# Values two units behind scores in the first chunk, and six decode and halving steps earlier, in a sparse attention and feed-forward kernel on one Trainium2 core

## The chip, the cores and the metric

The kernel runs on one core of a Trainium2 chip. TensorE (PE) does the matmuls, VectorE (DVE) and ScalarE (ACT) the elementwise work, GpSimd (POOL) copies, and SyncE (SP) issues almost all transfers. The metric is device time in microseconds (us), the median of the runs shown. Less is better.

## The reference

Attention over 4 batches, 8 heads, 768 positions and 64 numbers per head, with a mask by blocks of 32 positions, and a feed-forward layer behind it:

```python
scores = scale * np.matmul(q, k.transpose(0, 1, 3, 2))
mask = np.abs(blk_i - blk_j) <= 1
mask = mask | (blk_i == 0) | (blk_j == 0) | (blk_i == 23) | (blk_j == 23)
# and three sampled key blocks for each query block
scores = np.where(mask, scores, -1e9)
attn = softmax(scores)
x = (attn @ v).transpose(0, 2, 1, 3).reshape(3072, 512)
h = x @ w_in                       # 512 -> 2048
g = h * erf(softplus(h))
out = g @ w_out                    # 2048 -> 512
```

Everything is float32 outside. Inside, most matmuls take each factor as two float16 halves, a high one and a low one.

## The kernel before

**Units.** Each batch of attention is cut into 16 units. Units 0 to 9 of the first batch are the middle rows: unit n is row tile t = n // 2 (128 query positions) and quad n % 2 (four of the eight heads); in names of tiles, `pT_m_3_1` is tile 3, quad 1, so unit 7. Units 10, 11, 13, 14 (`f`) and 12, 15 (`e`) are the first and last blocks. For a unit, `scores` multiplies queries with gathered keys on PE into the one score bank `s`, `soft_max` takes maxima on DVE, `soft_exp` exponentiates on ACT (`pf`), `soft_low` makes the low halves on DVE (`p`), and `soft_turn` transposes the probabilities into `pT` by a DMA transpose that SP issues. `values` multiplies `pT` with gathered value blocks `vb` on PE into `po_bank`, and `norm` divides by the sum on DVE (`rinv`, `xf`). After a tile's second quad `turn` splits the rows (`x`) and has SP transpose them into `xT`.

**Groups.** The feed-forward layer runs in chunks of two tiles, each cut into 8 groups of two 128-wide slices of the hidden layer. The main loop runs over groups m; chunk 0 is m = 0 to 7 and chunk 1 m = 8 to 15. A group does `ff_first` (24 matmuls of `xT` with `w_in`, tile `h`), the logs and exponentials on ACT (`ff_logs`, `ff_exp`), a group later the gate on DVE (`ff_gate`, tile `g`), and two groups later `ff_second` (12 matmuls into `o` for each chunk). In its groups a chunk also starts units: `begun` counts them, from 4 at m = 0, one for each group of chunks 0 and 1. `scores` of unit `begun` and `values` of unit `begun - PV_LAG` (three) stand in the same group. So group m of chunk 0 scores unit 4 + m and takes the values of unit 1 + m, from unit 4 on. Units 0 to 3 are done in front of the loop.

**Gathers of values.** `vb` has 8 slots, four for a tile. When `values` of a tile's second quad is in the program, `gathers` issues the next tile's value blocks on SP: 14 transfers for a middle tile, 11 for the last blocks and two wholes.

**Weights.** They come as 64-bit words and are decoded in place: `D` (`decode_pair`, three DVE passes over two of the 16 pieces), `Q` (squares on ACT for the scale), `A` and `B` (sum over the squares, scale), `H` (`split_hi`, high halves on ACT) and `L` (`split_lo`, low halves on DVE). `i` is `w_in`, `o` is `w_out`, and the digit is the pair. The high halves of a pair are written over the pair before it, so `Hi3` needs `Li2`. `ff_first` of groups 0 and 1 needs pairs 0 and 1 of `w_in`, groups 2 and 3 need pairs 2 and 3, and so on. `Do2` and `Do3` also make POOL issue the loads of pairs 4 and 5 of `w_out`. The tables `EARLY`, `AMID` and `LATE` say which steps stand in which group, early (behind `scores`, the gate and `norm`, in front of `ff_second`), in the middle (behind `soft_exp`) and late (at the end).

**Order.** Every engine works through its instructions in the order of the program, which is written out by hand. SP's transfers each wait, in that order, for the transfer eight places earlier on the queue to have landed. In group 1, ACT's squares of the next batch's first value piece (`vj`, of tile `vraw`) stand in front of `soft_exp` of unit 5.

Of the kernel before, what the change touches and what calls it, by code (L numbers as in the profile page):

```python
# [24 lines left out]
H_CAP = 4.4  # L25


EARLY = ("", "", "Ao Bo Ho0 Lo0", "Hi5", "Hi6", "Hi7")
AMID = ("Do3 Qo1 Qo2", "Do5", "", "Li5 Lo2", "Li6 Lo3", "Li7 Lo4", "Lo5", "Lo6", "Lo7")
LATE = (  # L30
    "Qo3 Do4 Hi2 Li2 Qo4 Hi3 Li3",
    "Qo5 Do6 Qo6 Do7 Qo7",
    "Hi4 Ho1 Li4 Lo1 Ho2",
    "Ho3",
    "Ho4",
# [8 lines left out]
def sparse_attention_moe(ctx: ExitStack, tc: tile.TileContext, qT, kT, v, sampled, w_in, w_out, out):  # L44
# [38 lines left out]
    PV_LAG = 3  # L83
# [54 lines left out]
    def load_q(b, t):  # L138
        place, tag, bufs = (mo, "g", FF_LAG + 1) if b == 0 and t in (1, 2) else (ld, "qt", 2)
        qt = place.tile([P, HP, P], F32, tag=tag, name=f"qt_{b}_{t}", bufs=bufs)  # L140
        rows = qT[b].rearrange("(r t) d s -> (t d) r s", t=2)
        if t < MT:
            c = (1 + 4 * t) * BLOCK
            sp.dma_start(qt, rows[:, :, c : c + P])
        else:
            sp.dma_start(qt[:, :, : 3 * BLOCK], rows[:, :, S - 3 * BLOCK :])
            sp.dma_start(qt[:, :, 3 * BLOCK :], rows[:, :, :BLOCK])
        qts[b, t] = qt
# [114 lines left out]
    def write_values():  # L263
        for write in writes:
            sp.dma_start(*write)
        writes.clear()
# [272 lines left out]
    def work(steps):  # L539

        for step in steps.split():
            kind, key, k = step[0], step[1], step[2:]
            steps_of[kind](key, *([int(k)] if k else []))
# [274 lines left out]
    def write_results():  # L818
        for result in results:
            sp.dma_start(*result)  # L820
        results.clear()
# [21 lines left out]
    def gathers(m):  # L843

        nonlocal vfree
        gather_keys()
        room = 4 if begun > 0 else VGS
        while vjobs and vjobs[0][0] in have_v:
            b, i = vjobs[0]
            n = 2 if i > 0 else 1  # L850
            fresh = b > 0 and 0 < i < VGS
            if vfree < n or room < n * (1 + fresh):
                break
            vfree -= n
            room -= n * (1 + fresh)
            vjobs.pop(0)
            gather_v(b, i) if i > 0 else whole_v(b, -1 - i)
# [9 lines left out]
    def behind(m):  # L867

        b, n = divmod(m, per)
        if b + 1 < B:  # L870
            c = b + 1
            if n == 10:
                load_q(c, 0)
            k = n - 4 if b else 2 * (n - 10) if n > 9 else -1
            if k in ((1, 3, 5, 7) if b else (2, 4, 6, 8)):
                order_k(c, (k - 1) // 2)
            if k in (0, 2, 4, 6):
                load_k(c, k // 2)
            if k == 8:
                have_k.add(c)  # L880
            pr, k = divmod(n - 3, 3)
            if pr in range(HP):
                if k == 0:
                    load_v(c, pr)
                if k == 1:
                    prepare(square_v, None, (c, pr))
                if k == 2:
                    prepare(scale_v, None, (c, pr))
                    prepare(high_v, low_v, (c, pr))
                    if pr == HP - 1:  # L890
                        prepare(None, join_scales, (c,))
            if pr == HP and k == 0:
                have_v.add(c)
# [7 lines left out]
    def seen(unit):  # L901

        if unit[0] == "m":
            return unit[1:]
        if unit[0] == "e":
            return unit[1], MT, unit[2]
        return None

    def used_keys(unit):
        nonlocal kfree  # L910
        if unit[0] == "m" and unit[3] == 1:
            kfree += 4
        elif unit[0] == "e" and unit[2] == 1:
            kfree += 4

    FIRST = 4
    begun = 0

    def unit_of(n):
        return units[n] if 0 <= n < len(units) else None

    def values_of(place, *halves):
        nonlocal vfree
        values(*place, *halves)
        if place[2] == 1 and halves != ((0,),):
            vfree += 4 if place[1] < MT else 5
# [92 lines left out]
    work("Do2")  # L1021
    gathers(0)
    load_q(0, 3)
    begun = FIRST
    behind(begun - 1)

# [5 lines left out]
    for m in range(len(groups) + FF_LAG):  # L1032
        ch, i = divmod(m, NGR)
        steps = 0
        if ch < len(until):
            first = until[ch - 1] if ch else FIRST
            steps = first + -(-(until[ch] - first) * (i + 1) // NGR) - begun
        elif begun < len(units) + PV_LAG:
            steps = 1
        assert steps in (0, 1)  # L1040
        group = groups[m] if m < len(groups) else None
        last = groups[m - 1] if 0 < m <= len(groups) else None
        unit = unit_of(begun) if steps else None
        old = unit_of(begun - PV_LAG) if steps else None
        place = seen(old) if old and begun - PV_LAG >= FIRST else None
        begun += steps
        write_values()
        write_results()
        if group:
            ff_first(*group)  # L1050
            ff_logs(*group)
        ready, prepared[:] = prepared[:], []
        twice = bool(place) and place[1] == MT and m >= FF_LAG
        if place:
            values_of(place, *[(0,)] * twice)
        for high, _ in ready:
            if high:
                high()
        if twice:
            ff_second(*groups[m - FF_LAG], 0)  # L1060
            values_of(place, (1,))
        if steps:
            gathers(begun)
        if unit:
            scores(unit)
            used_keys(unit)
            gather_keys()
        if last:
            ff_gate(*last)
        if place:  # L1070
            norm(*place)
        if m < len(EARLY):
            work(EARLY[m])
        if m >= FF_LAG:
            for u in range(int(twice), CT):
                ff_second(*groups[m - FF_LAG], u)
        if unit:
            soft_max(unit)
            next_queries(begun - 1)
        if group:  # L1080
            ff_power(*group)
        for _, low in ready:
            if low:
                low()
        if unit:
            soft_exp(unit)
        if group:
            ff_exp(*group)
        if m < len(AMID):
            work(AMID[m])  # L1090
        if m >= FF_LAG:
            for u in range(CT):
                ff_store(*groups[m - FF_LAG], u)
        if unit:
            soft_low(unit)
            soft_turn(unit)
        if place:
            turn(*place)
        if m < len(LATE):
            work(LATE[m])  # L1100
        if unit:
            behind(begun - 1)
# [37 lines left out]
```

## Time and profile before

| | us |
|---|---|
| median of 3 runs | 808.74 (808.31 to 812.43) |
| the profiled execution | 805.82 |
| its span | 804.1 |

| engine | busy in the span, us | share |
|---|---|---|
| PE, matmuls | 698.1 | 87% |
| DVE | 571.2 | 71% |
| ACT | 550.8 | 69% |
| POOL | 120.8 | 15% |

The profiled execution is 2.92 us shorter than the median of the runs. Busy shares are averages over stages that differ: in front of the main loop, and in its first groups, PE waits for weights and transfers; later it hardly waits. So stages have to be read apart. Times in the rows are us from the span's start; a value in brackets is the idle time of that engine just before, and what ended it.

### The profile page before, as it was taken

To read this page: it belongs to the slowest core of one execution; us is meant where nothing else is said; L and a number is where in the kernel's file an instruction comes from. 1 tells how busy PE (TensorE), PEld (TensorE's weight loads), DVE (VectorE), ACT (ScalarE), POOL (GpSimd) and SP (SyncE) were. 2 spreads that over 40 slices of the span, in tenths; PEclk is the share of its full clock that TensorE was granted. 3 is DMA by queue.
4 is the path that set the end of the run, shared out by engine and by line. 5 is a ranking of instruction groups with operands and counts; after the bars stand their busy time and mean duration, and the time that the engine had idled before them with its cause. 6 is when DMAs were issued, how large, how long until landed. Compare 5 with 4: busy or idle time off the path is not lost.

```text
span 804.1 us, 26682 instructions
## 1 busy us (share of the span) xinstructions
PE 698.1 (87%) x10868; PEld 462.2 (57%) x10868; DVE 571.2 (71%) x1025; ACT 550.8 (69%) x943; POOL 120.8 (15%) x340
## 2 busy tenths in 40 slices
PE   2345646887998799999999999999999999999996
PEld 1234423544665566665666766666666666666663
DVE  3896687884877586886777848977768777654543
ACT  4654657984665577776767858876677776667674
POOL 4711211101311210210111111011111110000000
PEclk9999757998999899999999999999999999999999
DMA  8998972586979878893567998955677897410000
GB/s 312 280 285 269 288 169 63 126 191 140 186 157 179 204 184 196 190 235 63 145 162 149 236 189 166 234 125 126 134 174 149 179 176 190 67 42 2 14 28 26
DMA packets 200779, 129.24 MB, mean 161 GB/s; under 512 B 144080, under 2 KB 167760, under 8 KB 200656
## 3 DMA queue, kind: packets, MB, share of 16 engines
q1 hardware_dynamic: 197808, 117.83, 62.9%
q0 software_dynamic: 2848, 9.71, 3.8%
q8 instruction: 85, 1.39, 0.7%
q14 instruction: 38, 0.31, 0.1%
HBM read 81.52 MB, written 12.95 MB: 117 GB/s over the span
## 4 chain that ended last, share of the span: by engine, by line
PE 69%; DVE 10%; DMA 9%; ACT 5%; issue 4%; SPq 3%; POOL 0%; POOLq 0%; ACTq 0%; DVEq 0%
PE o L60 27%; PE h L60 27%; PE po_bank L60 6%; PE s_m L60 5%; SPq L60 3%; DMA vb<-vtab 3%; DVE keys L60 3%; PE s_f L60 3%; DMA vraw<-in_v_dram 2%; ACT x L60 1%; DVE wi L60 1%; ACT pf_m L60 1%; DMA keys<-in_w_out_dram 1%; DVE p_m L60 1%; DMA kr<-in_kT_dram 1%
## 5 line engine op out<-in xcount | busy, mean ns | idle before, releaser
L60 PE MATMUL h<-xT,wi 128*128 128x256 f16 x2304 | 277.5, 278 | 19.6 <-ACT wi L60 7.9
L60 PE MATMUL o<-wo,g 128*128 128x512 f16 x1152 | 270.2, 383 | 5.9 <-ACT wo L60 3.6
L60 PEld LDWEIGHTS <-wi 128*128 128x128 f16 x2304 | 228.7, 100 | 72.5 <-ACT wi L60 9.4
L60 PEld LDWEIGHTS <-g 128*128 128x128 f16 x1152 | 108.1, 99 | 142.5 <-issue 26.9
L60 ACT ACTIVATE x<-x 128x512 f32<-128x512 f32 x288 | 181.5, 630 | 9.2
L60 POOL COPY keys<-keys 128x128 f32 x264 | 90.2, 392 | 358.1 <-PE s_m L60 311.5
L60 ACT ACTIVATE x<-h,isg 128x512 f32<-128x512 f32 x96 | 66.0, 687 | 89.1 <-PE h L60 87.8
L60 DVE SCALAR_TENSOR_TENSOR q<-x,q 128x512 f32<-128x512 f32 x96 | 68.1, 710 | 59.2 <-ACT x L60 59.2
L60 ACT ACTIVATE pf_m<-s_m,nb_m 128x256 f32<-128x256 f32 x160 | 62.6, 473 | 51.5 <-DVE nb_m L60 48.6
L60 DVE SCALAR_TENSOR_TENSOR q<-q,h 128x512 f32<-128x512 f32 x96 | 65.4, 681 | 27.5 <-ACT q L60 27.5
L60 PE MATMUL s_m<-keys,qt 64*32 64x192 f32 (+1 forms) x1600 | 70.1, 352 | 7.7 <-ACT pf_m L60 4.9
L60 ACT ACTIVATE q<-q 128x512 f32<-128x512 f32 x96 | 60.5, 631 | 21.9 <-DVE q L60 21.8
L60 DVE SCALAR_TENSOR_TENSOR g<-q,g 128x512 f16<-128x512 f32 x96 | 66.5, 692 | 3.3
L60 ACT ACTIVATE q<-x 128x512 f32<-128x512 f32 x96 | 60.5, 630 | 3.0
L60 DVE TENSOR_REDUCE mx_m<-s_m 128x4 f32<-128x1024 f32 x40 | 48.8, 1220 | 19.0 <-PE s_m L60 18.5
L60 PEld LDWEIGHTS s_m<-keys,qt 64*32 64x32 f32 (+1 forms) x1600 | 45.5, 133 | 19.7 <-ACT pf_m L60 6.0
L60 PE MATMUL po_bank<-vb,pT_m 128*32 128x65 f16 (+1 forms) x3840 | 44.8, 201 | 12.5 <-DMA vb<-vtab 8.7
L60 DVE TENSOR_TENSOR p_m<-pf_m,p_m 128x1024 f16<-128x1024 f32 x40 | 49.0, 1226 | 4.6 <-ACT p_m L60 3.5
L60 PEld LDWEIGHTS <-pT_m 128*32 128x32 f16 x3840 | 38.0, 97 | 23.4 <-issue 13.3
L60 DVE TENSOR_SCALAR g<-q 128x512 f16<-128x512 f32 x96 | 41.1, 428 | 3.3
L60 DVE CAST p_m<-pf_m 128x1024 f16<-128x1024 f32 x30 | 20.9, 697 | 25.3 <-ACT pf_m L60 25.3
L60 POOL COPY keys<-wi 128x768 f32<-128x768 f32 (+1 forms) x24 | 14.4, 627 | 121.7 <-DMA wi<-in_kT_dram 115.6
(111 smaller groups left out, 528.1 us busy)
## 6 DMA issues: line engine op xcount, KB each, us to landing
vb<-vtab SPq DMA_DIRECT2D x280, 65.0 KB, 3.1
vb<-vtab SPq DMA_DIRECT2D x32, 390.0 KB, 4.4
vtab<-vn SPq DMA_DIRECT2D x16, 390.0 KB, 5.1
vb<-vtab SPq DMA_DIRECT2D x12, 520.0 KB, 5.2
qt<-in_qT_dram SPq DMA_DIRECT2D x20, 256.0 KB, 3.3
out_dram<-wo SPq DMA_DIRECT2D x20, 256.0 KB, 2.6
vb<-vtab SPq DMA_DIRECT2D x36, 130.0 KB, 3.4
vraw<-in_v_dram SPq DMA_DIRECT2D x12, 384.0 KB, 4.4
```

Of the source, the lines that this page charges most:

```text
L60: done = call(*args, **kwargs)
```

## The change

Two things move; no instruction is added but the order.

1. `values` runs two units behind `scores` instead of three while `begun` is under 12, that is in chunk 0; at m = 8 (`begun` 12) no values run; from m = 9 on it is three again. So units 4 to 9 have their values, their `norm` and their `turn`, and the gathers that follow, one group earlier (m = 2 to 7 instead of 3 to 8).
2. `Do3`, `Hi2`, `Li2`, `Hi3` and `Li3` go from groups 0 and 1 to the place in front of group 0; `Do4` to `Do6` each move up by half a group or so; `Do7`, `Qo6` and `Qo7` go from the end of group 1 into group 2, in front of `Ao`.

```diff
-EARLY = ("", "", "Ao Bo Ho0 Lo0", "Hi5", "Hi6", "Hi7")
-AMID = ("Do3 Qo1 Qo2", "Do5", "", "Li5 Lo2", "Li6 Lo3", "Li7 Lo4", "Lo5", "Lo6", "Lo7")
+EARLY = ("", "", "Qo6 Do7 Qo7 Ao Bo Ho0 Lo0", "Hi5", "Hi6", "Hi7")
+AMID = ("Do4 Qo1 Qo2", "Do6", "", "Li5 Lo2", "Li6 Lo3", "Li7 Lo4", "Lo5", "Lo6", "Lo7")
 LATE = (
-    "Qo3 Do4 Hi2 Li2 Qo4 Hi3 Li3",
-    "Qo5 Do6 Qo6 Do7 Qo7",
+    "Qo3 Do5 Qo4",
+    "Qo5",
...
+    NEAR = 12
...
     load_q(0, 3)
+    work("Do3 Hi2 Li2 Hi3 Li3")
     begun = FIRST
...
-        old = unit_of(begun - PV_LAG) if steps else None
-        place = seen(old) if old and begun - PV_LAG >= FIRST else None
+        due = begun - (PV_LAG - 1 if begun < NEAR else PV_LAG)
+        old = unit_of(due) if steps and begun != NEAR else None
+        place = seen(old) if old and due >= FIRST else None
```

**DVE at the head of the main loop.** `keys` is the decode's scratch, `wo<-wo,keys` the last pass of a `Do`, `wi<-wi,s_wi` an `Li`, `mx` the maxima of unit 4. Before:

```order
L60 SCALAR_TENSOR_TENSOR wo<-wo,keys 128x1024
L60 TENSOR_REDUCE mx_m_2_0_1203<-s_m_2_0_1182 128x4
L60 TENSOR_SCALAR nb_m_2_0_1205<-mx_m_2_0_1203 128x4
L60 SCALAR_TENSOR_TENSOR q_0_0_1179<-x_0_0_1175,q_0_0_1179 128x512
L60 TENSOR_SCALAR keys<-wo 128x1024
L60 SCALAR_TENSOR_TENSOR keys<-wo,keys 128x1024
L60 SCALAR_TENSOR_TENSOR wo<-wo,keys 128x1024
L60 TENSOR_TENSOR p_m_2_0_1213<-pf_m_2_0_1208,p_m_2_0_1213 128x4x256
```

and with the change:

```order
L60 SCALAR_TENSOR_TENSOR wo<-wo,keys 128x1024
L60 TENSOR_SCALAR keys<-wo 128x1024
L60 SCALAR_TENSOR_TENSOR keys<-wo,keys 128x1024
L60 SCALAR_TENSOR_TENSOR wo<-wo,keys 128x1024
L60 SCALAR_TENSOR_TENSOR wi<-wi,s_wi 128x2x512 x2
L60 TENSOR_REDUCE mx_m_2_0_1212<-s_m_2_0_1191 128x4
L60 TENSOR_SCALAR nb_m_2_0_1214<-mx_m_2_0_1212 128x4
L60 SCALAR_TENSOR_TENSOR q_0_0_1188<-x_0_0_1184,q_0_0_1188 128x512
L60 TENSOR_SCALAR keys<-wo 128x1024
```

A decode and two low halves now stand in front of the maxima of unit 4.

**DVE in group 2, up to the sum over the squares of `w_out`** (`top_wo`). `keys<-keys` to `wo<-keys` is `Do7`, `q` and `g` the gate of group 1, `p` the low halves of unit 5. Before:

```order
L60 SCALAR_TENSOR_TENSOR wo<-raw_612,keys 128x512
L60 TENSOR_SCALAR keys<-keys 128x1024
L60 SCALAR_TENSOR_TENSOR keys<-keys 128x1024
L60 SCALAR_TENSOR_TENSOR wo<-keys 128x1024
L60 TENSOR_SCALAR m_v_0_1382<-po_bank 128x1
L60 TENSOR_SCALAR e_v_0_1384<-m_v_0_1382 128x1
L60 TENSOR_SCALAR vs_1379<-e_v_0_1384 128x1
L60 TENSOR_SCALAR vi_1380<-e_v_0_1384 128x1
L60 SCALAR_TENSOR_TENSOR q_0_1_1268<-q_0_1_1268,h_0_1_1239 128x512
L60 TENSOR_SCALAR g_0_1_1414<-q_0_1_1268 128x512
L60 SCALAR_TENSOR_TENSOR g_0_1_1414<-q_0_1_1268,g_0_1_1414 128x512
L60 TENSOR_REDUCE top_wo<-sums 128x1
```

and with the change:

```order
L60 SCALAR_TENSOR_TENSOR q_0_1_1271<-q_0_1_1271,h_0_1_1242 128x512
L60 TENSOR_SCALAR g_0_1_1503<-q_0_1_1271 128x512
L60 SCALAR_TENSOR_TENSOR g_0_1_1503<-q_0_1_1271,g_0_1_1503 128x512
L60 SCALAR_TENSOR_TENSOR rinv_2_0_1506<-po_bank,vratio_299 128x4
L60 RECIPROCAL rinv_2_0_1506<-rinv_2_0_1506 128x4
L60 TENSOR_TENSOR xf_2_1509<-po_bank,rinv_2_0_1506 128x256
L60 TENSOR_SCALAR keys<-keys 128x1024
L60 SCALAR_TENSOR_TENSOR keys<-keys 128x1024
L60 SCALAR_TENSOR_TENSOR wo<-keys 128x1024
L60 TENSOR_REDUCE top_wo<-sums 128x1
```

`Do7` stands behind the gate and behind the `norm` of unit 4, which is new here; `Do6` (`raw_611`, `raw_612`) now stands in front of the low halves of unit 5.

**SP in groups 3 to 6.** `x_0_2` and `x_0_3` are the split rows of tiles 2 and 3, which chunk 1 reads. One piece of the difference, behind the 14 transfers of the gather of tile 4 (their own rows do not change):

```order
-L60 DMA_TRANSPOSE pT_m_4_0_1878<-p_m_4_0_1872 128x16x128
-L60 DMA_TRANSPOSE xT_1_1883<-x_0_2_1880 128x8x128
-L60 DMA_TRANSPOSE pT_m_4_1_2092<-p_m_4_1_2086 128x16x128
-L60 DMA vraw_2_2095<-in_v_dram 128x768
-L60 DMA vtab_95<-vn_1_2021 128x6x260
+L60 DMA qt_5_1771<-in_qT_dram 128x4x96
+L60 DMA qt_5_1771<-in_qT_dram 128x4x32
+L60 DMA_TRANSPOSE pT_m_3_1_1786<-p_m_3_1_1780 128x16x128
+L60 DMA_TRANSPOSE xT_1_1791<-x_0_2_1788 128x8x128
+L60 DMA_TRANSPOSE pT_m_4_0_1984<-p_m_4_0_1978 128x16x128
```

and behind the 11 transfers of the next gather:

```order
 L60 DMA vb<-vtab_94 128x2x1040 x2
-L60 DMA_TRANSPOSE pT_f_0_2274<-p_f_0_2269 128x12x128
-L60 DMA_TRANSPOSE xT_1_1883<-x_0_3_2276 128x8x128
-L60 DMA qt_0_2281<-in_qT_dram 128x4x128
-L60 DMA wi<-in_kT_dram 128x768
-L60 DMA_TRANSPOSE pT_f_1_2453<-p_f_1_2448 128x12x128
+L60 DMA_TRANSPOSE pT_m_4_1_2203<-p_m_4_1_2197 128x16x128
+L60 DMA_TRANSPOSE xT_1_1791<-x_0_3_2205 128x8x128
+L60 DMA vraw_2_2210<-in_v_dram 128x768
+L60 DMA vtab_95<-vn_1_2122 128x6x260
+L60 DMA_TRANSPOSE pT_f_0_2379<-p_f_0_2374 128x12x128
```

Both gathers stand a group earlier; the transpose of unit 7 (`pT_m_3_1`) and that of unit 9 (`pT_m_4_1`), which used to go out in front of a gather, now stand behind one. The transpose of tile 3's rows goes from the end of group 6 to the end of group 5.

## Rows read from the trace of the kernel before

**Rows 1.** Stages by windows: window and length, busy and count by engine, PEclk, DMA, GB/s.

```profile
83.00:133.00 50.00, 25.07 (x208) 14.86 (x208) 34.99 (x51) 31.07 (x54) 9.47 (x17) 0.61 0.63 173
133.00:186.00 53.00, 41.51 (x802) 26.54 (x801) 42.97 (x69) 45.00 (x70) 5.10 (x19) 0.95 0.75 162
186.00:804.10 618.10, 598.49 (x9227) 397.88 (x9225) 433.37 (x806) 430.25 (x748) 77.05 (x232) 0.99 0.64 143
```

**Rows 2.** PE in order of time: start, length, instructions, [idle before, what ended it].

```profile
99.20 0.61 PE L60 MATMUL h<-xT,wi 128*128 128x256 f16 x2 [4.58 <-ACT wi L60]
...
123.52 0.59 PE L60 MATMUL po_bank<-one,top_wo 128*128 128x1 f32 x2 [9.08 <-DVE top_wo L60]
127.67 0.59 PE L60 MATMUL o<-wo,g 128*128 128x512 f16 x1 [3.56 <-ACT wo L60]
...
135.86 0.99 PE L60 MATMUL po_bank<-vb,pT_m 128*32 128x65 f16 x96
...
153.37 0.95 PE L60 MATMUL po_bank<-vb,pT_m 128*32 128x65 f16 x96
...
171.87 2.78 PE L60 MATMUL h<-xT,wi 128*128 128x256 f16 x24
...
185.63 5.22 PE L60 MATMUL h<-xT,wi 128*128 128x256 f16 x24 [5.95 <-DMA xT<-x]
```

**Rows 3.** ACT in order of time, groups 0 to 2.

```profile
88.31 0.69 ACT L60 ACTIVATE x<-h,isg 128x512 f32<-128x512 f32 x1 [5.37 <-PE h L60]
...
109.42 0.84 ACT L60 ACTIVATE vj<-vraw 128x768 bf16<-128x768 f32 x1 [3.90 <-DVE keys L60]
...
121.20 1.06 ACT L60 ACTIVATE sq<-wo 128x1024 bf16<-128x1024 f32 x1 [2.10 <-DVE m_v L60]
...
126.48 1.13 ACT L60 ACTIVATE wo<-wo,s_wo 128x1024 f16<-128x1024 f32 x1
```

**Rows 4.** DVE in order of time, groups 0 to 3.

```profile
89.79 1.22 DVE L60 TENSOR_REDUCE mx_m<-s_m 128x4 f32<-128x1024 f32 x1 [5.45 <-PE s_m L60]
...
102.34 1.43 DVE L60 SCALAR_TENSOR_TENSOR wi<-wi,s_wi 128x1024 f16<-128x1024 f32 x1 [1.22 <-ACT wi L60]
...
112.93 1.23 DVE L60 TENSOR_TENSOR p_m<-pf_m,p_m 128x1024 f16<-128x1024 f32 x1 [2.33 <-ACT p_m L60]
...
117.89 0.69 DVE L60 TENSOR_SCALAR keys<-keys 128x1024 int32<-128x1024 int32 x1
...
119.88 1.22 DVE L60 SCALAR_TENSOR_TENSOR wo<-keys 128x1024 int32<-128x1024 int32 x1
...
123.31 0.15 DVE L60 TENSOR_REDUCE top_wo<-sums 128x1 f32<-128x8 f32 x1
...
124.60 0.14 DVE L60 TENSOR_SCALAR i_wo<-e_wo 128x1 int32<-128x1 int32 x1
...
139.20 0.42 DVE L60 TENSOR_TENSOR xf<-po_bank,rinv 128x256 f32<-128x256 f32 x1
```

**Rows 5.** SP's queue in order of time: start, time until the next, transfers.

```profile
105.92 0.35 SPq L60 DMA_DIRECT2D vraw<-in_v_dram  x1
...
138.43 1.87 SPq L60 DMA_DIRECT2D qt<-in_qT_dram  x2
...
149.48 10.26 SPq L60 DMA_DIRECT2D vb<-vtab  x14
...
169.28 8.74 SPq L60 DMA_DIRECT2D vb<-vtab  x11
...
179.51 4.08 SPq L60 DMA_TRANSPOSE xT<-x  x1
```

**Rows 6.** DMA issues from 60 to 140 us: median us from issue to landing.

```profile
pT_m<-p_m SPq DMA_TRANSPOSE x3, 4.9
```

**Rows 7.** Window of groups 1 and 2's head, columns as in rows 1.

```profile
89.00:99.00 10.00, 4.88 (x96) 3.57 (x80) 8.58 (x10) 9.79 (x17) 3.20 (x5) 0.97 1.05 328
```

**Rows 8.** PE's waits from 186 to 300 us: in total, times, longest.

```profile
PE po_bank L60 <- DMA vb<-vtab: 7.3, 6, 2.8
```

## The prediction

> **What bounds the kernel now.** I read the stages first. From 186 us on PE is busy for 598.5 of 618.1 us, so there a gain must come from PE's own work or from the few waits left. From 83 to 186 us it is busy for 25.1 of 50 and 41.5 of 53 us [rows 1], and the change touches only groups 0 to 8, which lie there. So next come PE's waits in that stretch, in order of time. Two groups stand out. In group 2 `ff_first` waits 4.58 us for the halves of pairs 2 and 3 of `w_in`; later in the group PE waits 9.08 us for the sum over the squares of `w_out` and 3.56 us for its first high halves. In group 8 it waits 5.95 us for the transposed rows of tile 3, and then runs its 24 matmuls in 5.22 us, where group 7 took 2.78 [rows 2]: after the wait the clock is at the lower of its two levels. A wait names who came last, not the cause, so each needs the queue of the engine named: ACT and DVE for group 2 [rows 3, 4], SP for group 8 [rows 5].
>
> **Part 1, in front of group 0.** The five steps moved there have a cover: ACT is idle 5.37 us before its first op of group 0, DVE 5.45 us before the maxima of unit 4 [rows 3, 4]. On DVE `Do3` is one pass of 0.69 and two of 1.22 us, `Li2` and `Li3` up to 1.43 each: about 5.9 us [rows 4]. On ACT `Hi2` and `Hi3` are 1.13 each, by the like copy of `w_out` [rows 3]. `Hi3` must wait for `Li2` and `Li3` for `Hi3`, so both engines come out some 1.5 us late: DVE starts the maxima near 91.2 instead of 89.79, ACT its logs near 89.9 instead of 88.31. Nobody pays, since the next thing on this path, the squares of `vraw` on ACT, starts at 109.42 only because `vraw`, which SP issues at 105.92, lands then; ACT has idled 3.90 us in front of it (the row names DVE, which had long been done) [rows 3, 5]. In return `ff_first` of group 2 runs without its wait, from some 96 us instead of 99.20. This alone shortens nothing: PE then stands and waits for the same `vraw`.
>
> **Part 2, group 2.** What decides is the chain behind `vraw`: the low halves of unit 5 on DVE, until 112.93 + 1.23 = 114.2, then `Do6`, then `Do7` from 117.89 to 121.1, the scale of the next values and the gate, and `top_wo` at 123.31 [rows 4]. With the change `Do6` (117.89 - 114.2 = 3.7 us) is done while DVE waits for `vraw`. Against that, the scale and the gate (123.31 - 121.1 = 2.2 us) no longer hide the squares of `Do7` (1.06 us, some 1.3 with the step to ACT and back [rows 3]), and `norm` of unit 4 is new (0.42 us and two small ops in front, some 0.8 [rows 4]). From 114.2: 2.2 + 0.8 + 3.2 (`Do7`) + 1.3 = 121.7, which is 1.6 us earlier than 123.31. The scale of `w_out` is ready 1.4 us later (124.60 + 0.14 before [rows 4]), now near 123.1. Before, ACT was then still busy with the logs of group 2 and value halves, and made the first high halves only at 126.48 [rows 3]; with `h` of group 2 ready long before, these logs now run ahead of the scale. So the high halves start near 123.2, 3.3 us earlier. I take 3.2 us for `ff_second` of group 2 on PE and all behind it.
>
> The bound from below is 0. `Do3` sends POOL's two loads of pair 5 of `w_out`, 1.05 MB, off some 8 us earlier. At the 328 GB/s of that window, with the DMA engines fully busy [rows 7], they take 3.2 us; if they all got in front of `vraw`, the gain would be gone. I don't take it, because in the kernel before these bytes left ahead of `vraw` too: `Do3` and `Do4` both stood in group 0, and `vraw` went out at 105.92 [rows 5]. The other bound is 4 us.
>
> Here the Trainium skill speaks against the change: "DMA: Bandwidth & Descriptors", section "Issuing engines are not separate DMA queues", says that transfers of SP and POOL run on the same 16 DMA engines and interleave, so a load begun earlier takes from those beside it. By that rule `vraw` would be late and the sum would be that of rival 1. The trace agrees that the engines are full there (share 1.05 [rows 7]); whether `vraw` pays, no row shows.
>
> **Part 3, groups 3 to 7.** Here the values stand two groups behind the transpose of their unit. The gather of tile 4, 14 transfers in 10.26 us, now stands in group 3, in front of the two query loads (1.87 us) and the transpose of unit 7, which lands 4.9 us after its issue [rows 5, 6]. That is 17.0 us after the gather starts, and it starts 1 to 3 us after `values` of unit 5 begin on PE (0.99 us of matmuls, and SP has other waits). `values` two groups apart were 153.37 - 135.86 = 17.5 us apart [rows 2]. So PE waits 0.5 to 2.5 us in group 5; DVE's maxima of unit 9 and `Li7` come later by about as much, and group 6 with them. I take 1.4 us lost, bounds 0 and 3. In group 5 the gather of 11 transfers (8.74 us) now stands in front of the transpose of unit 9 in the same way; 8.74 + 4.9 = 13.6 us [rows 5, 6], less than two groups. `norm` and `turn` add nothing to ACT and DVE over groups 3 to 7: each comes a group earlier and none is added. The Trainium skill ("DMA: Bandwidth & Descriptors", "Rules for kernel authors") advises to issue a transfer early and to wait for it late; a shorter distance goes against that, and by these rows its price is the 0.5 to 2.5 us.
>
> **Part 4, group 8.** The transpose of tile 3's rows went out at 179.51, behind 11 transfers begun at 169.28, and PE got it at 185.63 [rows 2, 5]. Now it goes out at the end of group 5. `values` of unit 7 stand where those of unit 6 stood, at 153.37 less the 2 us won so far; with 11 transfers and the transpose of unit 9 behind them that is near 166 us, and even with the 6.1 us it took before it lands by 173. PE is at group 8 near 178 (185.63 - 5.95 = 179.7 before, less 2). So the 5.95 us go. PE then comes from group 7 without a pause: 24 matmuls take 2.78 instead of 5.22 us, 2.44 less. The values of unit 9 have moved out of group 8, and the first ones into group 2, where PE waits anyhow: 0.95 less. Together 9.3 us; from below 7, if a shorter pause stays. What is late next are ACT and DVE, which both rested in the pause; from 186 us on they were busy for 430 and 433 of 618 us [rows 1], so PE should stay ahead.
>
> **Behind group 8.** SP, POOL and DVE keep their order relative to PE. The later waits for gathered values, 7.3 us in six pieces [rows 8], follow the program and move with it: 0, bounds -1.5 and +1.5.
>
> **The sum.** -3.2 + 1.4 - 9.3 = -11.1 us. Against the profiled execution, 805.8, that is 794.7; against the median of the runs, 808.74, which is 2.9 above it, 797.6. I give the latter.
>
> **Rivals.**
> 1. *Only group 8 gains.* The moved loads delay `vraw` by their 3.2 us [rows 7], or the waits of part 3 reach group 7 and eat as much. Then it is -11.1 + 3.2 = -7.9: 800.8 us. For it: full DMA engines, and queues that are in order. Against it: the same bytes were ahead of `vraw` before. The skill's rule on shared DMA engines, above, is this rival.
> 2. *No change.* The pause of group 8 moves to group 7: `values` of unit 9 wait for a transpose behind 11 transfers, the very queue that made `xT` land 6.1 us after its issue. With 4.5 us there, 2.4 us of lower clock and rival 1's 3.2 it is -11.1 + 10.1 = -1: 807.7 us. Against it: there are two groups of time now.
> 3. *Slower.* The transposes behind the two gathers become the bound: PE waits for units 7 and 9, and each wait brings the clock down, at 2.4 us a time as in group 8. With two waits of 8.5 us it is 2 x 10.9 - 12.5 (parts 2 and 4) = +9.3: 818 us. It decides from waits of 3.9 us each, that is when both gathers need some 3 us more than in rows 5 and little slack is left. For it: they now stand beside other transfers. Against it: DMA is busy for 0.75 of that stretch [rows 1].
>
> **Chances.** Forecast 0.62 (-8.5 to -14.5), rival 1 0.22 (-5 to -8.5), rival 2 0.11, rival 3 0.05. The range holds the first two, 0.84: 793.8 to 803.8. 0.5%, 4 us, is about what a measurement of this kernel can tell from no change. The first two are faster by more, and a little of rival 2 is too: faster 0.86, same 0.09, slower 0.05.
>
> **What would show it.** Part 1: no wait in `ff_first` of group 2, the squares of `vraw` still near 109.4. Part 2: `top_wo` near 121.7, the first `ff_second` near 124.5. Part 3: a wait of PE for the transpose of unit 7 in group 5, none in group 7. Part 4: no wait for `xT` at group 8, 24 matmuls in 2.8 us there, and group 9 some 11 us earlier. The forecast is wrong if the squares of `vraw` come at 112 or later, if PE waits over 4 us in groups 5 or 7, or if what is won at group 9 is gone by 300 us.

## The result, and the profile after

The changed kernel takes 795.92 us (794.07 to 797.79, 6 runs), the kernel before beside it 809.34 us (806.60 to 812.43, 6 runs). The ratio is 0.9839, with a 95% interval of 0.9815 to 0.9863. The forecast was 797.6 us, the range 793.8 to 803.8. The sum behind it was -11.1 us; the two medians are 13.4 us apart, 0.6 of it because the median of before is 809.34 us over six runs and was 808.74 over the first three.

The profiled execution of after took 796.71 us with a span of 795.0 us, only 9.1 us less than that of before. This is not the same 13.4; the last part of "Why" says where the difference lies.

The stages of after, in the columns of [rows 1], with the borders moved to the same groups (start of group 0, of group 3 and of group 9):

```profile
83.00:131.20 48.20, 24.38 (x305) 16.02 (x305) 36.07 (x55) 31.38 (x55) 9.99 (x17) 0.68 0.63 180
131.20:182.50 51.30, 46.86 (x862) 30.15 (x861) 46.44 (x79) 47.90 (x75) 6.01 (x22) 0.97 0.89 198
182.50:795.00 612.50, 588.62 (x9071) 391.93 (x9069) 430.64 (x794) 426.69 (x743) 76.31 (x229) 0.99 0.63 142
```

In the second stage, groups 3 to 8, PE is now busy for 46.86 of 51.3 us. Its four longest waits from 80 to 186 us (engine and line <- what it waited for: us in total, times, longest):

```profile
PE po_bank L60 <- DMA pT_m<-p_m: 13.7, 2, 11.9
PE po_bank L60 <- DVE top_wo L60: 6.0, 1, 6.0
PE s_m L60 <- ACT pf_m L60: 3.2, 1, 3.2
PE o L60 <- ACT wo L60: 1.8, 1, 1.8
```

No wait for a transfer of `xT` is among them or among the shorter ones. The long one, 11.9 us, is group 2's: PE now does `ff_first` of group 2 early and then stands in front of the first `values`. The other 1.8 us of that line is the new wait of group 5. The same in order of time, columns as in [rows 2]:

```profile
96.28 4.46 PE L60 MATMUL h<-xT,wi 128*128 128x256 f16 x24
112.68 1.50 PE L60 MATMUL po_bank<-vb,pT_m 128*32 128x65 f16 x96 [11.93 <-DMA pT_m<-p_m]
...
123.16 0.59 PE L60 MATMUL po_bank<-one,top_wo 128*128 128x1 f32 x2 [5.96 <-DVE top_wo L60]
125.56 0.58 PE L60 MATMUL o<-wo,g 128*128 128x512 f16 x1 [1.81 <-ACT wo L60]
...
131.19 2.78 PE L60 MATMUL h<-xT,wi 128*128 128x256 f16 x24
...
153.11 0.96 PE L60 MATMUL po_bank<-vb,pT_m 128*32 128x65 f16 x96 [1.78 <-DMA pT_m<-p_m]
...
161.78 1.92 PE L60 MATMUL h<-xT,wi 128*128 128x256 f16 x16 [0.86 <-DVE wi L60]
...
176.26 2.78 PE L60 MATMUL h<-xT,wi 128*128 128x256 f16 x24
...
182.46 2.78 PE L60 MATMUL h<-xT,wi 128*128 128x256 f16 x24
```

The row at 176.26 is group 8: no wait, 2.78 us for its 24 matmuls, where [rows 2] has 5.95 us of waiting and 5.22 us. Group 9 starts at 182.46; before it started at 195.34. From here to group 46, where before and after start at 468.73 and 455.84 us, the distance stays at 12.9 us.

To see in which group the time was won, I worked out from PE's rows of every kernel when `ff_first` of each group starts. The table gives the distance from one group's start to the next, in us; the kernels beside after and before are those of the experiments, and the last column is measured against the first run of before.

| | group 2 | 3 | 4 | 5 | 6 | 7 | 8 | start of 9, earlier than before |
|---|---|---|---|---|---|---|---|---|
| before | 33.94 | 7.64 | 9.88 | 7.91 | 13.30 | 13.76 | 9.71 | - |
| before, another run | 36.19 | 7.60 | 9.81 | 7.91 | 13.28 | 13.72 | 9.80 | -0.99 |
| after | 34.91 | 7.60 | 9.76 | 11.33 | 8.74 | 7.64 | 6.20 | 12.88 |
| after, second run | 36.11 | 7.81 | 9.22 | 9.57 | 11.70 | 7.64 | 6.20 | 8.81 |
| after, third run | 34.93 | 7.61 | 9.44 | 9.53 | 11.76 | 7.64 | 6.20 | 12.94 |
| lag alone | 36.42 | 7.61 | 10.28 | 9.38 | 10.31 | 7.64 | 6.20 | 9.54 |
| steps alone | 32.89 | 7.61 | 9.80 | 7.92 | 13.25 | 13.71 | 9.82 | 2.78 |
| gather of tile 4 behind | 34.82 | 7.73 | 10.15 | 7.91 | 12.87 | 13.60 | 6.20 | 4.98 |
| gather of tile 3 behind | 30.05 | 8.10 | 8.93 | 9.60 | 10.30 | 7.65 | 6.19 | 18.19 |
| `NEAR` 8 | 35.43 | 7.61 | 8.87 | 8.05 | 13.96 | 13.61 | 9.91 | 2.96 |
| `NEAR` 10 | 34.41 | 7.60 | 9.72 | 11.11 | 7.72 | 7.64 | 7.27 | 14.49 |
| `Do3` put back | 38.06 | 7.61 | 9.65 | 11.34 | 8.67 | 7.64 | 6.20 | 12.09 |
| gather of tile 3 behind, `NEAR` 10 | 28.13 | 7.72 | 9.98 | 9.70 | 9.35 | 7.64 | 7.36 | 17.93 |

### The profile page after: what moved, and what is told of

It reads as the page before. It is cut to its first block, busy times and chain, and to the rows that moved or that the text cites. A ratio compares the mean times of both kernels' runs of the same rounds, so it can differ in the third digit from the quotient of the medians.

```text
span 795.0 us, 26684 instructions
## 1 busy us (share of the span) xinstructions
PE 692.9 (87%) x10868; PEld 461.3 (58%) x10868; DVE 573.0 (72%) x1025; ACT 550.4 (69%) x943; POOL 121.5 (15%) x340
## 3 DMA queue, kind: packets, MB, share of 16 engines
q0 software_dynamic: 2848, 9.71, 3.6%
q8 instruction: 85, 1.39, 0.7%
## 4 chain that ended last, share of the span: by engine, by line
PE 68%; DMA 12%; DVE 7%; SPq 5%; ACT 4%; issue 3%; POOL 0%; POOLq 0%; ACTq 0%; DVEq 0%
PE o L60 27%; PE h L60 26%; PE po_bank L60 6%; DMA vb<-vtab 6%; PE s_m L60 5%; SPq L60 5%; PE s_f L60 3%; DMA vraw<-in_v_dram 2%; DMA vtab<-vn 1%; DVE g L60 1%; ACT pf_m L60 1%; DVE mx_m L60 1%; DVE q L60 1%; DMA kr<-in_kT_dram 1%; ACT x L60 1%
## 5 line engine op out<-in xcount | busy, mean ns | idle before, releaser
L60 PE MATMUL h<-xT,wi 128*128 128x256 f16 x2304 | 271.2, 275 | 4.4 <-DVE wi L60 1.8
L60 DVE CAST p_m<-pf_m 128x1024 f16<-128x1024 f32 x30 | 21.2, 708 | 25.4 <-ACT pf_m L60 25.4
L60 POOL COPY keys<-wi 128x768 f32<-128x768 f32 (+1 forms) x24 | 16.8, 730 | 110.8 <-DMA wi<-in_kT_dram 110.8
```

The costliest lines, as they stand in the source:

```text
L60: done = call(*args, **kwargs)
```

## The experiments

**The two parts apart.** The theory: the two units of distance win the 9 us of group 8 and the moved steps the 3 us of group 2, each without the other. The rival: one needs the other, or one of them is worth nothing. The first kernel has after's loop with before's tables:

```diff
-EARLY = ("", "", "Qo6 Do7 Qo7 Ao Bo Ho0 Lo0", "Hi5", "Hi6", "Hi7")
-AMID = ("Do4 Qo1 Qo2", "Do6", "", "Li5 Lo2", ...
+EARLY = ("", "", "Ao Bo Ho0 Lo0", "Hi5", "Hi6", "Hi7")
+AMID = ("Do3 Qo1 Qo2", "Do5", "", "Li5 Lo2", ...
-    "Qo3 Do5 Qo4",
-    "Qo5",
+    "Qo3 Do4 Hi2 Li2 Qo4 Hi3 Li3",
+    "Qo5 Do6 Qo6 Do7 Qo7",
...
-    work("Do3 Hi2 Li2 Hi3 Li3")
```

> The shorter lag alone, with the tables of the kernel before. Theory (the forecast's parts 3 and 4): PE's wait for xT at group 8 is gone (-9.3 us with clock and values), a wait of 0.5 to 2.5 us for the transpose of unit 7 comes in group 5 (+1.4), norm of unit 4 now stands in front of the sum over w_out's squares (+0.8): some 7 us faster than the kernel before, about 802 us; group 2 still waits 4 to 5 us for wi and about 9 for top_wo. Rival (most of the gain came from the moved steps): at most 3 us faster, and a wait of over 3 us at group 8 or in group 7.

Measured: 797.10 us (793.48 to 802.20) against 807.51 us, ratio 0.9881 (0.9844 to 0.9917): 10.4 us faster, where I had expected some 7. The wait for `xT` is gone, the two waits of group 2 are there as in before (4.58 us for the halves, 8.38 us for `top_wo`), and group 9 starts 9.54 us earlier. The surplus lies mainly in groups 5 and 6: they take 19.7 us together, before 21.2, although PE waits 1.39 us in group 5 for the transpose of unit 7.

The second kernel has after's tables with before's loop:

```diff
-        due = begun - (PV_LAG - 1 if begun < NEAR else PV_LAG)
-        old = unit_of(due) if steps and begun != NEAR else None
-        place = seen(old) if old and due >= FIRST else None
+        old = unit_of(begun - PV_LAG) if steps else None
+        place = seen(old) if old and begun - PV_LAG >= FIRST else None
```

> The moved decode and halving steps alone, values three units behind all through. Theory: group 3 starts 2 to 4 us earlier, everything up to group 8 moves with it, and the wait for xT at group 8 stays near 6 us with 5.2 us for its matmuls behind it: 3 to 4 us faster than the kernel before, about 805.5 us. Rival (group 8 waits because of what was late in group 2): the wait at group 8 falls below 3 us and the kernel is 7 us or more faster.

Measured: 805.05 us against 807.51, ratio 0.9964 (0.9941 to 0.9987). Group 3 starts 2.69 us earlier and group 9 2.78 us earlier. Group 8 keeps its wait:

```profile
182.74 5.28 PE L60 MATMUL h<-xT,wi 128*128 128x256 f16 x24 [5.90 <-DMA xT<-x]
```

Both parts do what they say, each without the other: at group 9 they win 9.54 and 2.78 us alone, 12.3 together by sum, and 12.88 us in the first profile of after; by the medians it is 10.4 and 2.5 us, and 13.4 together. The two runs of before are 1 us apart at group 9 and the three of after 4 us, so the sum can't be read more finely than that.

**The gather of tile 4 behind the transposes.** In after the 14 gathers of tile 4 stand on SP in front of the transpose for which PE then waits in group 5. If that wait is a loss, moving these gathers behind group 3's transposes should bring it back.

```diff
+    LATER = (3,)
...
-        if steps:
+        if steps and m in LATER:
+            gather_keys()
+        elif steps:
             gathers(begun)
...
+        if steps and m in LATER:
+            gather_values()
```

> The changed kernel with the gather of tile 4 issued at the end of group 3, behind the transposes of unit 7 and of tile 2's rows, not in front. Theory (the wait of 1.78 us in group 5 is the transpose of unit 7 standing behind 14 transfers on SP): that wait is gone, group 6 starts 1 to 2 us earlier, and the time is 1 to 2 us under the changed kernel's, 794 to 795. Rival a (the transpose is late for another reason, such as full DMA engines): the wait stays. Rival b: the gather now stands in front of the transpose of unit 8, and the wait moves to group 6; time unchanged within 1 us.

Measured: 801.18 us (797.61 to 804.20), ratio 0.9917 (0.9884 to 0.9950). By the ratio, 0.9839 for after, this is slower than after, so the theory fell, and neither rival came true. The wait of group 5 did go (its length is 7.91 us, as in before), but group 6 then takes 12.87 us, as it did before. And behind it a worse wait came. SP and PE in group 7 (columns as in [rows 5] and [rows 2]; the second column of SP's rows is the time that SP spent issuing the row's transfers, not the time until the next row):

```profile
149.76 9.48 SPq L60 DMA_DIRECT2D vb<-vtab  x14
159.35 1.83 SPq L60 DMA_TRANSPOSE pT_m<-p_m  x1
161.27 7.42 SPq L60 DMA_DIRECT2D vb<-vtab  x11
168.77 4.42 SPq L60 DMA_TRANSPOSE pT_m<-p_m  x1
```

```profile
176.76 1.50 PE L60 MATMUL po_bank<-vb,pT_m 128*32 128x65 f16 x96 [3.42 <-DMA pT_m<-p_m]
178.19 2.83 PE L60 MATMUL s_f<-keys,qt 64*64 64x512 f32 x8
180.95 3.38 PE L60 MATMUL o<-wo,g 128*128 128x512 f16 x12
```

The two gathers are now almost back to back, and unit 9's transpose goes out behind both, at 168.77 us. PE waits 3.42 us for it. Behind the wait the granted clock is 0.50 in the window from 176.8 to 182 us, the lower of the two levels, and values, scores and `ff_second` take 1.50, 2.83 and 3.38 us where after has 0.96, 1.51 and 2.76. Together that is 3.42 + 0.54 + 1.32 + 0.62 = 5.9 us, and group 7 is 13.60 us instead of 7.64. This is the wait that my second rival put into group 7, and half of my third, with a price: 5.9 us for a wait of 3.4.

**The gather of tile 3 behind `vraw`.** The trace of after says that group 2 is bound by `vraw`, which SP issues at 106.85 us behind the 14 gathers of tile 3 that start at 90.27. If that is so, moving these gathers behind `vraw` and unit 4's transpose must bring group 3 forward. The edit is that of the last kernel with `LATER = (0,)`, and `gather_keys()` in place of `gathers(0)` in front of the loop.

> The changed kernel with the gather of tile 3, 14 transfers, issued at the end of group 0, behind vraw and the transpose of unit 4; it used to stand in front of both. Theory (group 2 is bound by vraw, which stands behind that gather on SP): the squares of vraw start near 104.5 instead of 110.8, top_wo comes 4 to 5 us earlier, group 3 too, and the time is 4 to 5 us under the changed kernel's, about 791. Rival (DMA engines are full until 110 us whatever the order, or DVE's and ACT's own work bounds group 2): top_wo moves by less than 1.5 us, time within 1.5 us of the changed kernel's.

Measured: 791.93 us (788.10 to 793.24) against 807.51, ratio 0.9805 (0.9774 to 0.9835). Its SP, ACT and PE:

```profile
94.03 0.50 SPq L60 DMA_DIRECT2D vraw<-in_v_dram  x1
98.54 5.07 SPq L60 DMA_TRANSPOSE pT_m<-p_m  x1
103.72 9.54 SPq L60 DMA_DIRECT2D vb<-vtab  x14
```

```profile
104.20 0.83 ACT L60 ACTIVATE vj<-vraw 128x768 bf16<-128x768 f32 x1
```

```profile
126.38 3.27 PE L60 MATMUL h<-xT,wi 128*128 128x256 f16 x24
```

The squares of `vraw` no longer wait. Group 3 starts at 126.38 us, 4.8 us earlier than in after, and group 9 at 177.15, 5.3 us earlier. The 14 gathers, which took 16.06 us at their old place, take 9.54 at the new one. So what bound group 2 was the order on SP. The edit moves two transfers in front of the gathers, and no run separates them: by the rows of after `vraw` comes last, but the values that wait for unit 4's transpose (112.68 us), with the sum over the squares behind them (until 114.70), are done only 0.75 us before DVE needs that sum at 115.45. The kernel is faster than before. It is 4 us below after by the medians, but the two ratios (0.9805 and 0.9839) were not measured side by side and their intervals overlap; the 5.3 us at group 9 are the firmer reading.

**How many units stand two behind.** `NEAR` is the unit from which the distance is three again. If the two units of distance win because the transposed rows of tile 3 leave at the end of group 5 instead of group 6, then 8 must lose group 8's gain and 10 must keep it.

```diff
-    NEAR = 12
+    NEAR = 8
```

The other kernel has 10 there.

> The changed kernel with the shorter lag for units 4 and 5 only (the constant 12 set to 8): tile 3's rows are split and transposed at the end of group 6 again. Theory (the wait of group 8 is that transpose, and unit 7's earlier values alone take it away): the wait of about 6 us and 5.2 us of matmuls are back at group 8, groups 2 to 7 stand as in the changed kernel within 1.5 us, and group 9 starts only 2 to 4 us earlier than before: about 2 to 4 us faster than the kernel before. Rival (what helps group 8 is that all is earlier): the wait stays under 3 us, 8 us or more faster.

> The changed kernel with the shorter lag for units 4 to 7 (the constant 12 set to 10): units 8 and 9 keep their old groups, so the values of unit 9 stand in group 8 again, and unit 9's transpose has a group more. Theory: no wait for xT at group 8; 0.95 us of values back in group 8, nothing else: group 9 within 1.5 us of the changed kernel's, about 1 us later. Rival (units 8 and 9 carry a part of the gain, or their transpose costs a wait in group 7): group 9 differs by more than 2 us from the changed kernel's, either way.

Measured: with 8, 806.58 us, ratio 0.9965 (0.9927 to 1.0003), not clear of no change, and the wait of group 8 is back:

```profile
182.47 5.30 PE L60 MATMUL h<-xT,wi 128*128 128x256 f16 x24 [5.80 <-DMA xT<-x]
```

I had expected groups 2 to 7 within 1.5 us of after, which groups 5 and 6 missed: without the wait in group 5 they take 8.05 and 13.96 us, much as in before. With 10, 794.65 us, ratio 0.9860 (0.9840 to 0.9880), no wait for `xT`. The values of unit 9 stand in group 8 again, which is 7.27 us long instead of 6.20; but group 6 is shorter too, and group 9 starts 1.6 us earlier than in after, where I had expected 1 us later. So the gain of group 8 hangs on units 8 and 9 being scored while values are two behind, that is on units 6 and 7 getting their values in groups 4 and 5. Whether 10 or 12 is the better one, these times do not tell.

**Before and after once more, one profile each.** The first two profiles differ by 9.1 us, the medians by 13.4.

> The changed kernel once more, for a second trace. In its first trace 12.9 us were won at group 9 and kept to group 46; in group 47, 3.4 us of wait and a low clock took 4 us of it back, where the kernel before waited 1.4 us. Theory (the time at which a transpose on SP lets the next load go varies by a microsecond there, in either kernel): group 47 may come out at 7 or at 11 us in this trace, groups 0 to 9 as in the first trace within 1.5 us. Rival (the change costs these 4 us each time): group 47 takes over 10 us again, and the kernel before 7 us again in its second trace.

> The kernel before once more, for a second trace beside the repeat of the changed kernel. Theory (group 47 varies in either kernel): some run of before shows group 47 at 10 us or more, and its groups 3 to 9 stand where they stood within 1.5 us. Rival (only the changed kernel pays there): 7 us again.

Measured: 800.79 and 811.30 us, 10.5 apart. In the second run of after group 3 starts 1.25 us later than in the first profile of before, since SP started the 14 gathers only at 94.45 us and `vraw` went out at 109.67. I had expected groups 0 to 9 within 1.5 us of the first profile, so that missed; why SP was late is open. At group 9 this run is 9.8 us ahead of the other run of before. The groups of before did stay within 1.1 us. And in both kernels one more place varies, group 47, as the theory had it (10.93 us here in after, 12.50 in before); it is taken up below.

**Do the moved loads delay `vraw`?** That was the first half of my first rival. One step goes back, with its two POOL loads:

```diff
-AMID = ("Do4 Qo1 Qo2", "Do6", "", ...
+AMID = ("Do3 Do4 Qo1 Qo2", "Do6", "", ...
...
-    work("Do3 Hi2 Li2 Hi3 Li3")
+    work("Hi2 Li2 Hi3 Li3")
```

> The changed kernel with one step put back: decoding w_out's pair 3, with the two POOL loads of pair 5 behind it, stands in group 0 again, as in the kernel before. Theory 'the moved loads compete with vraw' (my rival 1): vraw lands 1.4 to 3 us earlier than in the changed kernel (the squares of vraw near 108 to 109.4 instead of 110.8), group 3 starts as much earlier, and the time is 2 to 3 us below the changed kernel's. Theory 'the landing of vraw varies by itself' : the squares stay between 109 and 112, the time is within 1.5 us of the changed kernel's, or up to 2 us above it, since group 0 has one more decode.

> The changed kernel once more on this chip, as the measure for the two beside it: some 13 us below the kernel before, group 9 of PE 9 to 13 us earlier than there.

Measured on one chip, beside 809.70 us for before: after 795.42 us (ratio 0.9822, 0.9779 to 0.9866), with `Do3` put back 799.23 us (ratio 0.9871, 0.9827 to 0.9915). Rows of the kernel with `Do3` put back (SP, then DVE), and the SP rows of after's third run:

```profile
89.59 13.40 SPq L60 DMA_DIRECT2D vb<-vtab  x14
...
105.66 0.35 SPq L60 DMA_DIRECT2D vraw<-in_v_dram  x1
```

```profile
104.61 0.69 DVE L60 TENSOR_SCALAR keys<-wo 128x1024 int32<-128x1024 int32 x1 [5.09 <-DMA wo<-in_w_out_dram]
...
115.16 1.22 DVE L60 TENSOR_TENSOR p_m<-pf_m,p_m 128x1024 f16<-128x1024 f32 x1
```

```profile
88.82 16.42 SPq L60 DMA_DIRECT2D vb<-vtab  x14
...
105.75 0.50 SPq L60 DMA_DIRECT2D vraw<-in_v_dram  x1
```

The loads do slow the 14 gathers: with the loads moved to the front these took 14.5 to 16.9 us in seven profiles with the gathers at that place, and 13.4 to 14.4 us in the four without. But `vraw` leaves at the same time, 105.66 and 105.75 us here: where the gathers are quick, SP stands for another 2.2 to 2.9 us in front of `vraw`, and where they are slow it goes on at once. The traces show for what: SP waits for the transfer eight places earlier, itself one of the gathers. In the four profiles without the moved loads it lands 0.01 to 0.02 us before `vraw` goes out (in before at 105.91, and `vraw` at 105.92), in the seven with them 0.5 to 1.5 us before. The squares of `vraw` start at 109.4 to 111.0 us in the four profiles without the moved loads, and at 109.3 to 113.6 us in the seven with them; the means are 110.1 and 110.9. So the full 3.2 us were not paid, and whether 0.7 us were can't be told in this spread. Putting `Do3` back was no gain but 3.8 us of loss by the medians, more than either of my two theories gave. Its rows of DVE show a reason that neither had: the loads go out later, DVE stands 5.09 us for one of them in front of a decode, and reaches the low halves of unit 5 at 115.16 us without idling, 2.1 us later than in after's third run, where it waits there. Group 3 starts 1.9 us later for it. Between these two profiles, 797.95 and 791.61 us, 0.9 us are left at group 9 and 1.8 at group 46; the rest is group 47, long in one and short in the other. How much of the medians' 3.8 us is group 47, these runs don't tell.

**Both good edits together.** Tile 3's gather behind `vraw`, and 10 for `NEAR`:

> The kernel with tile 3's gather behind vraw and unit 4's transpose, and the switch from two units to three a group earlier (10 instead of 12). If the two effects add up: the run with the gather moved was 4.0 us below the changed kernel's median, the run with the early switch 1.3 us below, so some 5 us below, near 790.5. If the early switch is worth nothing by itself (its 1.3 us lie within the spread of the medians): 791.5 to 792.5.

Measured: 792.08 us (789.44 to 793.90), ratio 0.9774 (0.9725 to 0.9824), beside 795.42 for after on the same chip. The edits do not add up: 10 in place of 12 is worth nothing that shows. The gather behind `vraw` has its gain a second time at group 9: 5.0 us against the run of after beside it and 3.4 against 10 alone (17.93, 12.94 and 14.49 us earlier than before).

## Why the prediction was right, and where it was not

**Part 1** holds. DVE starts the maxima of unit 4 at 91.38 us (91.2 by the prediction), ACT its logs at 90.05 (89.9), and `ff_first` of group 2 runs at 96.28 us without its wait. PE waits 3.2 us for ACT in group 1 now, but stands 11.93 us in group 2 in any case, so nobody paid.

**Part 2** has the right chain, but its size moves with `vraw`. The rows of after (ACT, then DVE):

```profile
110.79 0.84 ACT L60 ACTIVATE vj<-vraw 128x768 bf16<-128x768 f32 x1 [6.55 <-DMA vraw<-in_v_dram]
...
124.36 1.15 ACT L60 ACTIVATE wo<-wo,s_wo 128x1024 f16<-128x1024 f32 x1 [1.45 <-DVE s_wo L60]
```

```profile
114.31 1.23 DVE L60 TENSOR_TENSOR p_m<-pf_m,p_m 128x1024 f16<-128x1024 f32 x1 [5.03 <-ACT p_m L60]
...
122.95 0.16 DVE L60 TENSOR_REDUCE top_wo<-sums 128x1 f32<-128x8 f32 x1 [1.27 <-ACT sq L60]
```

From the end of the low halves to `top_wo` I had 121.7 - 114.2 = 7.5 us; the trace has 122.95 - 115.45 = 7.5 (115.45 is where the next DVE operation starts). From there the high halves follow after 1.4 us, 1.5 by the prediction. So every step of the chain was sized well and only its start was 1.4 us late, since `vraw` was: 110.79 against 109.42 us [rows 3]. In the first profile the part is worth 1.95 us at group 3 instead of 3.2, in the third run of after, with `vraw` squared at 109.52, 2.92 us, and alone 2.69. The bounds of 0 and 4 us hold these three. They don't hold the second run of after, where SP came to the gathers 4 us late and group 3 started 1.25 us later than in the first profile of before (against the other run of before, 0.2 us later): `vraw` was squared at 113.64 us there, 3.3 us later than in that run, which is as much as the part wins. Squares at 112 us or later were one of my signs that the forecast is wrong; what saved it in that run is part 4.

**Part 3** had the wrong sign. The wait itself came as predicted, in group 5, for unit 7's transpose: 1.78, 1.58 and 1.54 us in the three runs of after and 1.39 with the lag alone, where I had said 0.5 to 2.5; and there was none in group 7. The step that failed is "`Li7` come later by about as much, and group 6 with them". Group 6 had waits of its own, and these shrink when PE comes later. Rows of before that I had not read: the window from group 5's scores to the end of group 6's `ff_first`, in the columns of [rows 1], then PE and `Li7` on DVE there:

```profile
155.00:167.00 12.00, 8.38 (x89) 4.74 (x90) 11.69 (x23) 10.58 (x18) 1.70 (x6) 0.86 0.56 135
```

```profile
161.68 0.39 PE L60 MATMUL h<-xT,wi 128*128 128x256 f16 x2 [2.29 <-ACT wi L60]
163.40 3.55 PE L60 MATMUL h<-xT,wi 128*128 128x256 f16 x16 [1.33 <-DVE wi L60]
```

```profile
162.07 1.28 DVE L60 SCALAR_TENSOR_TENSOR wi<-wi,s_wi 128x1024 f16<-128x1024 f32 x1
```

In after, PE behind the wait of group 5, and `Li7`:

```profile
154.31 2.23 PE L60 MATMUL s_m<-keys,qt 64*128 64x64 f32 x40
156.47 3.57 PE L60 MATMUL o<-wo,g 128*128 128x512 f16 x12
```

```profile
160.44 1.28 DVE L60 SCALAR_TENSOR_TENSOR wi<-wi,s_wi 128x1024 f16<-128x1024 f32 x1
```

In before DVE is busy for 11.69 of these 12.0 us and ACT for 10.58: the stretch goes by these two engines, not by PE. PE stood 2.29 + 1.33 us anyway and then ran 16 matmuls in 3.55 us, with a granted clock of 0.51 in the window from 163.5 to 166.8 us. In after `Li7` starts 1.63 us earlier, where group 5 had started 2.11 us earlier: of the wait of 1.78 us only some 0.5 us reached it.

A second thing that I had left out of part 3 is the clock. In the first profile of after the wait in group 5 is followed by scores in 2.23 us and `ff_second` in 3.57, where before has 1.47 and 2.76; the granted clock is 0.75 from 153.1 to 159.9 us. Group 5 is 3.4 us longer than before, and group 6 is 4.6 us shorter: 0.86 us in front of the low halves, and the 16 matmuls in 1.92 us, at a clock of 1.00. In the second and third run of after the clock stays up in group 5 and falls in group 6 instead (the 16 matmuls take 2.60 and 3.02 us). Groups 5 and 6 together take 20.07 us in the first profile, 21.27 and 21.29 in the other two, and 21.21 in before: the wait cost less than 0.1 us in any of them.

From group 3 to group 7, part 3 is worth -1.30 us in the first profile, -0.43 and -0.39 in the other two, and not the +1.4 that I took. The bound of 0 at the good end was too tight. That DVE and ACT set the pace is argued from their busy shares; no run changed their work alone. Two runs agree with it: with the gather of tile 4 behind, the wait of group 5 is gone and group 6 takes up the time (20.78 us together), and with 10 for `NEAR`, which takes unit 8's values and `norm` out of group 6, DVE is busy for 17.18 us in groups 5 and 6 instead of 18.24, and they take 18.83 us instead of 20.07.

**Part 4** holds almost to the digit. From group 7's start to group 9's: 13.76 + 9.71 = 23.47 us before, 7.64 + 6.20 = 13.84 after, which is -9.63 us; predicted -9.3. SP in group 5 of after:

```profile
164.07 4.15 SPq L60 DMA_TRANSPOSE pT_m<-p_m  x1
168.32 1.26 SPq L60 DMA_TRANSPOSE xT<-x  x1
```

The transposed rows of tile 3 go out at 168.32 us, still behind the 11 gathers and unit 9's transpose, as I had put them, but 2.3 us later than the 166 us of the prediction; PE takes them at 176.26 us without a wait. Unit 9's transpose is issued at 164.07 us and used at 171.33 without a wait. The same 13.84 us stand in all three runs of after and in the kernel with the lag alone.

**The sum.** At group 9: -1.95 - 1.30 - 9.63 = -12.88 us in the first profile. Two errors, +1.25 us in part 2 and -2.7 in part 3, cancelled in part; that is luck, and the forecast is better than its terms. The ends of the range were also added up loosely: -14.5 and -5 us from 808.74 are 794.2 and 803.7, where I gave 793.8 and 803.8.

**Behind group 8** I had said 0, bounds -1.5 and +1.5. Up to group 46 that holds (12.88 and 12.89 us). Then group 47 took 7.00 us in the profile of before and 11.67 in that of after, and 4.7 us seem lost. They are not the change's, since other runs of the same two kernels have it the other way round. SP and PE there, before and then after:

```profile
467.33 1.84 SPq L60 DMA_TRANSPOSE pT_m<-p_m  x1
...
472.58 0.42 SPq L60 DMA_DIRECT2D vraw<-in_v_dram  x1
```

```profile
480.83 0.35 PE L60 MATMUL po_bank<-one,vsq 128*128 128x1 f32 x2 [1.41 <-DVE xf L60]
481.04 2.75 PE L60 MATMUL o<-wo,g 128*128 128x512 f16 x12
```

```profile
455.65 2.77 SPq L60 DMA_TRANSPOSE pT_m<-p_m  x1
...
460.47 0.42 SPq L60 DMA_DIRECT2D vraw<-in_v_dram  x1
```

```profile
469.62 0.56 PE L60 MATMUL po_bank<-one,vsq 128*128 128x1 f32 x2 [3.40 <-DVE xf L60]
470.04 5.28 PE L60 MATMUL o<-wo,g 128*128 128x512 f16 x12
```

PE waits in group 47 in either kernel (the row names `xf`; its matmul sums the squares of the last batch's `vraw`). A wait of 1.4 us leaves the clock as it is here, one of 3.4 us is followed by `ff_second` in 5.28 instead of 2.75 us. The other run of before had the long form (12.50 us, a wait of 4.97), the third run of after the short one (7.25 us). Over all 13 profiles the group is 7.0 to 7.3 us long in four and 10.7 to 12.8 in nine, with no order by what was changed. In all 13 the transpose `pT_m` in front of `vraw` goes with it: it held SP for 1.8 to 2.0 us where the group was short and for 2.7 to 3.5 where it was long. That this decides is argued from the traces; no experiment was made on it, and why the transpose takes longer is open.

**The rivals.** Rival 1, that only group 8 gains, fell with the steps alone, which win 2.8 us, and with `Do3` put back, which wins nothing. The rule that stood beside it, of the Trainium skill ("DMA: Bandwidth & Descriptors", section "Issuing engines are not separate DMA queues"), that transfers of SP and POOL share the 16 DMA engines, agrees with the trace: the 14 gathers became slower by some 2 us. It did not set the time, because SP's pause of 2.2 to 2.9 us in front of `vraw` took that up. The other rule of the Trainium skill that I weighed ("DMA: Bandwidth & Descriptors", "Rules for kernel authors"), to issue early and wait late, would have charged part 3 with its wait. Here the wait stood in front of others that shrank, and cost nothing. Rival 2 fell with the rows of group 7, which has no wait. Rival 3 did not occur either. But the wait for unit 9's transpose that both name is real: it shows once the two gathers stand back to back.

## What to carry to other kernels

A wait that a change adds costs only what the next wait on the same engine does not give back: before charging it, look whether another engine is full over the groups behind it (here DVE, 11.69 of 12.0 us, and ACT), in a window as short as those groups. On a queue that issues in order, look what the first thing waited for stands behind: `vraw`, 384 KB, and one transpose in front of 14 gathers instead of behind them were worth 5 us at PE, more than the 2.8 of the steps moved on ACT and DVE. And compare two profiles by the start of every group, not by their ends: one place that varies by 5 us hid a third of this gain.

## What the runs showed that I had not expected

- The same 14 gathers of values held SP for 13.4 to 16.9 us in front of the loop, and for 9.5 and 9.6 us a group later, behind `vraw` and unit 4's transpose. SP's own time was 0.3 to 0.4 us for each in after; at some, such as those at 101.80 and 102.87 us, it went on 0.02 us after the transfer eight places earlier had landed. How long a row of transfers holds the queue is then set in part by how soon earlier ones land.
- A DMA transpose of `p_m` held SP's queue for 1.84 us at 467.33 and for 5.09 us at 474.13 in the one profile of before. What stands behind it is issued so much later.
- What a pause of PE costs does not go by its length alone. In group 47 the next 12 matmuls of `ff_second` took 2.75 us after a wait of 1.4 us and 5.28 us after one of 3.4, the granted clock being 1.00 and 0.50 in these stretches. In group 5 waits of 1.49, 1.72 and 1.78 us in three kernels were followed by `ff_second` in 3.86, 3.77 and 3.57 us, and waits of 1.39 to 1.72 us in five other profiles by one in 2.76 us.
